# Adding raw x to ten blocks of the state at fold time, and storing those blocks straight from the state

## The chip, the cores and the metric

The kernel runs on one core of a Trainium2 chip. The metric is the time of one execution on the device in microseconds (us), the median of three runs. Engines are named as the profile names them: PE is the matrix engine and PEld its weight loads, DVE the vector engine, ACT the scalar engine, POOL the GpSimd engine, and SP the engine that issues all of this kernel's DMAs. Each engine works through its own queue of instructions in order.

## What is computed

Two branches read the same 2048 x 448 input, and their sum is added to it:

```python
def reference(A_x, A_w_r, A_w_i, B_x, B_w1, B_w2, B_w3, B_w4):
    def _A_ref(x, w_r, w_i):
        X = rfft2(x) * (w_r + 1j * w_i)
        return irfft2(X, s=(S, D))
    def _B_ref(x, w1, w2, w3, w4):
        h = _gelu(_layernorm(x, axis=-1) @ w1)
        hs = concatenate([four shifts of quarters of h], axis=-1) @ w2
        x1 = x + hs
        h2 = _gelu(_layernorm(x1, axis=-1) @ w3) @ w4
        return x1 + h2
    x = A_x
    xn = _layernorm(x, axis=-1)
    return x + _A_ref(xn, A_w_r, A_w_i) + _B_ref(xn, B_w1, B_w2, B_w3, B_w4)
```

Here S is 2048, D is 448 and the hidden width of the second MLP is 1792. B_x is not read. What matters for the change is the last line: raw x is one of three terms of the result, and terms may be added in any order as long as each is in the right scale.

## The kernel before

**Tiling.** The 2048 rows are cut into 16 blocks of 128 rows, row a*16+b being row a of block b. Each block has a slot of 128 x 448 floats in SBUF, `xb(b)`, which lives in the four tiles `xt`. It starts as x, is normalised in place, and from then on holds the running sum of the result: this is the state. To keep the half-precision matmuls in range, the state of blocks 0 to 11 is carried in a scaled form until the end; the factor `p12` (a column of the small tile `s12`) turns it back, and what is added to it on the way is multiplied to match: `p34[:,0:1]` is the scale for adding the MLP's result to a scaled state, `p34[:,1:2]` the one for adding it to an unscaled row, and `sc[:,1:2]` the one for adding the spectral result to a scaled state.

**Stages.** First the token mixing (w1, shifts, w2), to about 98 us. Then the channel MLP, in eight groups G of two blocks, each in seven steps fp. A step has a `front` (22 matmuls at L433 into a bank `pw`, the gelu at L763, the split of the result into two halves `hf` by ACT at L767 and DVE at L768) and a `back` (12 or more matmuls at L798 and L809 into the accumulators); fronts run up to two steps ahead of backs. After the last step DVE adds the accumulator to the state (L818). The MLP is the filler of the whole second part of the kernel: the spectral branch is laid into it. That branch has a fold stage (`do_fold`, about 98 to 186 us), a stage of 16 spectral chunks (about 190 to 270 us) and an inverse stage (about 280 to 381 us).

**The fold stage** goes by pairs of blocks b0 = 0, 2, ..., 14. For each pair SP loads the raw x again into a buffer `xf` of which there are three (L571), ACT normalises it in place (L575, L576), POOL folds it with four additions through `xr` (L580 to L583), ACT and DVE split it into halves `xh` (L591, L592), PE transforms it (`step1`, L601), and ACT and DVE copy the result out of its bank (L605, L606). On POOL the fold shares the queue with `w4_forms` (L897 to L901), which prepares weights.

**The inverse stage** goes over the blocks in the order 12 to 15, 8 to 11, 0 to 7. `gather_u` and `inv_a` (L716 to L739) prepare a block, and `inv_b` multiplies it (L746) and adds it to the state on DVE (L747). For blocks below 12, `finish` follows: raw x is loaded a third time into one of two rows of `xr` (L556), DVE forms state * p12 + x there (L557), and SP stores the row (L561). Because there are two rows, a load waits until the store two blocks earlier is done. Blocks 12 to 15 get their raw x in a separate place ahead of the last two MLP groups, also by L556 and L557, and are stored at the very end.

**Order.** Nobody writes the order of the queues out by hand. A planner simulates the engines and puts ready instructions into the queues by priority: the MLP's matmuls have the lowest (`FILL`), its evacuations the highest (`EVAC`), the rest lies between in the order of the program. `with behind(key)` holds an instruction back, in the plan, until the instructions that were recorded under that key have been issued. `("f", G, fp)` is the split of `front(G, fp)` on ACT and DVE, `("m", G, fp)` the last matmul of `back(G, fp)`. `FOLD[b0 // 2]` is such a key for each pair: (0,5), (1,0), (1,1), (1,3), (1,4), (1,6), (2,0), (2,2).

Of the kernel before, what the change touches and what calls it, by code (L numbers as in the profile page):

```python
# [16 lines left out]
ALU = mybir.AluOpType  # L17
AX = mybir.AxisListType

S, D, DF, F = 2048, 448, 225, 1792  # L20
# [15 lines left out]
WMAX = [(1, 4), (1, 5), (2, 0), (2, 0), (2, 1), (2, 2), (2, 3), (2, 4)]  # L36
LATE = [(2, 2), (2, 3), (2, 4), (2, 5)]
HS = 3
STR = (5, 6, 7)
INV, LAG = 4, 2  # L40
EVAC, FILL = 0, 100000
# [81 lines left out]
def body(tc, nc, x, wf, w1, w2, w3, w4, c_g, c_n, c_small, out):  # L123
# [41 lines left out]
    def xb(b):  # L165
        g, i = WHERE[b]
        return xt[g][:, i]
# [385 lines left out]
    def unscaled(b, t=None):  # L553
        if t is None:
            t = row()[:, :D]
        SY.dma_start(t, xv[:, b])  # L556
        V.scalar_tensor_tensor(out=t, in0=xb(b), scalar=p12, in1=t, op0=ALU.mult, op1=ALU.add)  # L557
        return t

    def finish(b):  # L560
        SY.dma_start(ov[:, b], unscaled(b))  # L561


    OFF = [0, 113, 225, 338, 450]
    FAM = [0, 2, 1, 3]
    folds = {}

    def do_fold(b0):
        f = pfd.tile([128, 2, 4, 113], F32, tag="xf", bufs=3, name=f"xf{b0}")
        X = f.rearrange("p b s d -> p (b s d)")[:, 0:2 * D + 2].rearrange("p (b d) -> p b d", b=2)  # L570
        after["X", b0] = (SY.dma_start(X[:, :, 0:D], xv[:, b0:b0 + 2]).ins,)  # L571
        with behind("f", *FOLD[b0 // 2]):
            for i in range(2):
                x_ = X[:, i, 0:D]
                A.activation(out=x_, in_=x_, func=AF.Identity, scale=xn_scale[b0 + i], bias=xn_bias[b0 + i])  # L575
            A.activation(out=X[:, :, D:D + 1], in_=X[:, :, 0:1], func=AF.Copy)  # L576
        ad = X[:, :, 0:D].rearrange("p b (h d) -> p h b d", h=2)[:, :, :, 0:113]
        bc = X[:, :, 1:D + 1].rearrange("p b (h d) -> p h b d", h=2)[:, ::-1, :, 223:110:-1]
        u = xr.rearrange("p (a b s d) -> p a b s d", a=2, b=2, s=2)
        P.tensor_tensor(out=u[:, 0], in0=ad, in1=bc, op=ALU.add)  # L580
        P.tensor_tensor(out=u[:, 1], in0=ad, in1=bc, op=ALU.subtract)
        for k, op in ((0, ALU.add), (2, ALU.subtract)):
            i = P.tensor_tensor(out=f[:, :, k:k + 2].rearrange("p b s d -> p s b d"), in0=u[:, :, 0], in1=u[:, :, 1], op=op)  # L583
        after["fold", b0] = (i.ins,)
        for i in range(2):
            folds[b0 + i] = f[:, i].rearrange("p s d -> p (s d)")
# [33 lines left out]
    def w_scale_end(wm):  # L620
        t = pc.tile([128, 4], F32, name="wt")
        V.tensor_reduce(out=t[:, 0:1], in_=wm, axis=AX.X, op=ALU.max)
        pt = bank("sp", "wpt")
        T.transpose(pt[0:1, 0:128], t[:, 0:1], ident)
        V.tensor_reduce(out=t[0:1, 1:2], in_=pt[0:1, 0:128], axis=AX.X, op=ALU.max)
        V.tensor_scalar(out=t[0:1, 1:2], in0=t[0:1, 1:2], scalar1=2.0 ** -20, scalar2=None, op0=ALU.max)
        pb = bank("sp", "wpb")
        T.matmul(pb[:, 0:1], ones[0:1], t[0:1, 1:2], start=True, stop=True)
        e = pc.tile([128, 3], I32, name="we")
        V.tensor_copy(out=t[:, 2:3], in_=pb[:, 0:1])  # L630
        V.tensor_single_scalar(e[:, 0:1], t.bitcast(I32)[:, 2:3], 0x7F800000, op=ALU.bitwise_and)
        V.tensor_single_scalar(e[:, 1:2], e[:, 0:1], 0x7F800000, op=ALU.bitwise_xor)
        V.tensor_scalar(out=sc[:, 0:1], in0=e.bitcast(F32)[:, 1:2], scalar1=ZPRE, scalar2=None, op0=ALU.mult)
        for h in range(2):
            V.tensor_scalar(out=sc[64 * h:64 * h + 64, 2:3], in0=sc[64 * h:64 * h + 64, 0:1], scalar1=2.0 * h - 1.0,
                            scalar2=None, op0=ALU.mult)
        V.tensor_scalar(out=sc[:, 1:2], in0=e.bitcast(F32)[:, 0:1], scalar1=2.0 ** -21 / (ZPRE * UPRE * VPRE),
                        scalar2=s12[:, 0:1], op0=ALU.mult, op1=ALU.mult)


    stream, pfs, zs = {}, {}, {}
# [100 lines left out]
    def inv_b(b):  # L742
        vh = vhs.pop(b)
        py = bank("sp", f"py{b}")
        for n, (vi, ri) in enumerate(PASS):
            T.matmul(py[:, :D], cV[ri], vh[:, vi], start=n == 0, stop=n == 2)  # L746
        V.scalar_tensor_tensor(out=xb(b), in0=py[:, :D], scalar=sc[:, 1:2], in1=xb(b), op0=ALU.mult, op1=ALU.add)  # L747


    acc, xs, hs, hg, rest = {}, {}, {}, {}, {}  # L750
# [27 lines left out]
    def back(G, fp):  # L778
        h = hs.pop((G, fp))
        n = D // 2  # L780
        end = 4 if G == 7 else 6
        if fp == 0:
            acc[G] = [bank("acc", f"acc{G}{i}") for i in range(2)]
            if G in STR:
                xs[G] = [bank("tr", f"cr{G}{i}") for i in range(2)]
        if (G, fp) == (7, 5):
            xs[G] = [bank("tr", f"end{i}") for i in range(2)]
        C = [[(slice(0, D), acc[G][i][:, 0:D], 0, 6)] for i in range(2)]
        if G == 7:
            C[1] = [(slice(0, D), acc[G][1][:, 0:D], 0, 4)]  # L790
            if fp > 4:
                C[1] = [(slice(n * k, n * k + n), xs[G][k][:, 0:n], 5, 6) for k in range(2)]
        for i in range(2):
            for r, to, s, e in C[i]:
                with behind("m", G, fp) if (G, fp) == (7, 6) and ("m", G, fp) in after else contextlib.nullcontext():
                    for f in range(2):
                        for hi, wi in ((0, 0),) if crossed(G, fp) else ((0, 0), (0, 1), (1, 0)):
                            m = T.matmul(to, h[:, hi, 2 * f + i], w4p[0][:, wi, 2 * fp + f, r],  # L798
                                         start=fp == s and f == 0 and hi + wi == 0, stop=fp == e and f == 1 and hi == 1)
                after["m", G, fp] = (m.ins,)  # L800
        if crossed(G, fp):
            g = hg.pop((G, fp))
            X = [xs[G][k // 2][:, n * (k % 2):n * (k % 2) + n] for k in range(4)]
            H = [[acc[G][i][:, n * k:n * k + n] for k in range(2)] for i in range(2)]
            forms = [(0, 1, X[0], 9), (1, 3, H[1][0], 9), (3, 2, H[0][0], C[0][0][3]), (6, 4, X[2], 9),
                     (4, 5, X[3], end), (5, 6, X[1], end), (2, 7, H[1][1], C[1][0][3])]
            for hi, wi in ((0, 1), (1, 0)):
                for k, slot, to, e in forms:
                    m = T.matmul(to, h[:, hi, slot] if slot < 4 else g[:, hi, slot - 4], w4f[fp][k][wi], start=k in (0, 6) and fp == 0 and hi == 0,  # L809
                                 stop=hi == 1 and fp == e)  # L810
            after["m", G, fp] = (m.ins,)
        k34 = p34[:, 1:2] if G >= 6 else p34[:, 0:1]
        to = {i: rest[2 * G + i] if G >= 6 else xb(2 * G + i) for i in range(2)} if fp >= 4 else {}

        def evacuate(i):
            for r, src, _, e in C[i]:
                if fp == e:
                    V.scalar_tensor_tensor(out=to[i][:, r], in0=src, scalar=k34, in1=to[i][:, r], op0=ALU.mult, op1=ALU.add)  # L818
                    if G == 7 and fp == 6:
                        SY.dma_start(ov[:, 2 * G + i, r], to[i][:, r])  # L820

        with prio(EVAC):
            if G in STR and fp == end:
                e0, e1 = cross[:, 0], cross[:, 1]
                for i in range(2):
                    A.activation(out=cross[:, i], in_=xs[G][i][:, 0:D], func=AF.Copy, scale=k34)
                for o, x, y in ((e0[:, n:], e0[:, 0:n], e0[:, n:]), (e1[:, 0:n], e1[:, 0:n], e0[:, n:]),
                                (e0[:, n:], e0[:, n:], e1[:, n:]), (e1[:, n:], e1[:, 0:n], e1[:, n:])):
                    (V if G == 7 else P).tensor_tensor(out=o, in0=x, in1=y, op=ALU.add)
            for i in range(2):  # L830
                evacuate(i)
                if G in STR and fp == end:
                    (V if G == 7 else P).tensor_tensor(out=to[i], in0=to[i], in1=cross[:, 1 - i], op=ALU.add)
                if G == 6 and fp == 6:
                    SY.dma_start(ov[:, 2 * G + i], to[i])
# [235 lines left out]
    xh_buf = [pfd.tile([128, 2 * 452 + 16], F16, name=f"xh{i}") for i in range(4)]  # L1071
    for i in range(4):
        P.memset(xh_buf[i][:, 904:], 0.0)
    mlp([1, 2], ahead=AH, tags=("mm", "tr"))
    for b in range(0, NB, 2):
        do_fold(b)
        step1_in(b)
        step1_in(b + 1)
        with behind("m", *PACE[b // 2]):
            step1(b)  # L1080
            step1(b + 1)
# [74 lines left out]
```

## Time and profile before

| what | value |
|---|---|
| median of three runs | 410.98 us (409.61, 410.98, 411.87) |
| the profiled execution | 411.11 us, of which the profile's span is 409.2 us |
| granted clock of the matrix engine | 1.0 throughout |
| busy share of the span: PE, DVE, ACT, POOL | 98%, 77%, 66%, 40% |
| share of the chain that ended last: PE, DVE, ACT, DMA | 68%, 12%, 7%, 6% |

The chain is followed backwards from the last instruction, at each step to what released it. Busy shares are means over stages with different limits, so the views that follow are read stage by stage. A row of the timeline has the start in us, the duration in us, the engine, the line of the kernel, the operation, the tiles written and read, shapes, and a count; a bracket at its end gives the engine's idle time before the row and what ended it. A row with a count above one is a run of instructions whose duration reaches from the first start to the last end.

### The profile page before, as it was taken

The numbers are of one execution on the slowest core, as the hardware profiler recorded it, in microseconds if no ns is written. First come the engines' busy times: TensorE is split into PE (matmuls) and PEld (weight loads), VectorE is DVE, ScalarE is ACT, GpSimd is POOL, SyncE is SP. The second block draws the span as 40 slices with busy tenths as digits, with TensorE's granted clock in tenths as the row PEclk, the third lists the DMA queues.
The fourth block names the chain that finished last, engine by engine and source line by source line (L and its number), as shares of the span: only waits on it lengthen the run. The fifth ranks groups of instructions, "written<-read, shape, count | busy, mean of one in ns | idle before, by whom it ended". The sixth has DMA issues, their size and how long they took to land.

```text
span 409.2 us, 8827 instructions
## 1 busy us (share of the span) xinstructions
PE 402.4 (98%) x3379; PEld 295.4 (72%) x3379; DVE 313.3 (77%) x674; ACT 268.2 (66%) x465; POOL 164.1 (40%) x260
## 2 busy tenths in 40 slices
PE   8999999999999999999999999999999999999996
PEld 3554555666677877677878887877788888878885
DVE  5989998898654737975899988841698969898645
ACT  4699993984838766754788888757566555644332
POOL 3889820002297745599321212100133234434300
PEclk9999999999999999999999999999999999999999
DMA  8999999907710356527367567320000202332201
GB/s 280 352 264 181 170 178 259 270 2 156 159 48 0 94 207 198 158 24 179 94 173 157 144 149 181 98 60 2 1 2 2 69 22 77 107 108 76 88 2 45
DMA packets 57209, 49.46 MB, mean 121 GB/s; under 512 B 41312, under 2 KB 52192, under 8 KB 57168
## 3 DMA queue, kind: packets, MB, share of 16 engines
q1 hardware_dynamic: 57168, 48.91, 46.3%
q8 instruction: 26, 0.43, 0.4%
q14 instruction: 15, 0.12, 0.1%
HBM read 35.06 MB, written 3.67 MB: 95 GB/s over the span
## 4 chain that ended last, share of the span: by engine, by line
PE 68%; DVE 12%; ACT 7%; DMA 6%; issue 3%; POOL 1%; SPq 0%; ACTq 0%; DVEq 0%; POOLq 0%
PE pw L433 23%; PE acc L798 18%; PE pw L462 6%; PE pw L507 6%; PE cr L809 3%; DMA wl<-wf 2%; PE acc L809 2%; ACT te L680 2%; PE ps L601 2%; PE py L746 2%; PE pe L724 2%; DVE te L683 1%; DVE te L681 1%; PE pu L704 1%; DMA h<-hs 1%
## 5 line engine op out<-in xcount | busy, mean ns | idle before, releaser
L433 PE MATMUL pw<-x2mem,w3p 128*128 128x256 f16 x1232 | 151.4, 272 | 0.0
L433 PEld LDWEIGHTS <-w3p 128*128 128x128 f16 x1232 | 118.8, 98 | 18.4
L798 PE MATMUL acc<-w4p,hf 128*128 128x448 f16 x508 | 106.7, 352 | 0.2 <-DVE xt L818 0.2
L798 PEld LDWEIGHTS <-hf 128*128 128x128 f16 x532 | 51.6, 98 | 37.1 <-issue 0.4
L768 DVE SCALAR_TENSOR_TENSOR hf<-pw,h,hf 128x512 f16<-128x512 f32 x56 | 41.8, 747 | 35.3 <-ACT hf L767 35.0
L763 ACT ACTIVATE pw<-pw,pe 128x512 f32<-128x512 f32 x56 | 36.7, 655 | 42.5 <-PE pw L433 42.4
L731 POOL TENSOR_TENSOR e<-e 128x226 f32<-128x226 f32 x16 | 12.8, 801 | 72.0 <-ACT e L728 67.9
L767 ACT ACTIVATE hf<-pw,h 128x512 f16<-128x512 f32 x56 | 38.3, 685 | 1.3
L507 PE MATMUL pw<-w2p,h 112*128 112x448 f16 x192 | 38.9, 352 | 0.1
L685 POOL TENSOR_TENSOR xr<-te 128x450 f32<-128x450 f32 x16 | 16.2, 1012 | 56.5 <-DVE te L683 50.6
L462 PE MATMUL pw<-w1p,w4x 128*128 128x448 f16 x176 | 34.9, 352 | 0.5 <-DVE h L936 0.5
L507 PEld LDWEIGHTS <-h 112*128 112x128 f16 x192 | 18.5, 98 | 16.8 <-DMA h<-x2mem 0.8
L462 PEld LDWEIGHTS <-w4x 128*128 128x128 f16 x176 | 17.0, 98 | 16.5 <-ACT w4x L422 0.7
L728 ACT ACTIVATE e<-pe 128x452 f32<-128x452 f32 x16 | 8.7, 544 | 20.7 <-PE pe L724 20.7
L580 POOL TENSOR_TENSOR xr<-xf 128x452 f32<-128x452 f32 x8 | 8.9, 1109 | 27.0 <-issue 16.0
L716 ACT ACTIVATE U<-y 113x512 f16<-113x512 f16 x32 | 18.0, 619 | 0.0
L592 DVE TENSOR_TENSOR xh<-xf,xh 128x452 f16<-128x452 f32 x16 | 14.0, 907 | 5.0 <-ACT xh L591 5.0
L680 ACT ACTIVATE te<-px 64x450 f32<-64x450 f32 x32 | 17.3, 539 | 0.6
L583 POOL TENSOR_TENSOR xf<-xr 128x452 f32<-128x452 f32 x16 | 16.7, 1066 | 0.6
L809 PE MATMUL cr<-w4x,hg 128*128 128x224 f16 x102 | 15.8, 259 | 0.1
L809 PEld LDWEIGHTS <-hg 128*128 128x128 f16 x152 | 14.7, 98 | 1.2 <-DVE hg L772 0.5
L738 ACT ACTIVATE vh<-e 128x448 f16<-128x448 f32 x16 | 9.2, 573 | 8.8 <-DVE e L736 8.8
(201 smaller groups left out, 773.1 us busy)
## 6 DMA issues: line engine op xcount, KB each, us to landing
wc<-wf SPq DMA_DIRECT2D x32, 225.0 KB, 3.7
wl<-wf SPq DMA_DIRECT2D x8, 450.0 KB, 3.7
xf<-x SPq DMA_DIRECT2D x8, 448.0 KB, 3.6
xt<-x SPq DMA_DIRECT2D x3, 896.0 KB, 11.0
w3raw<-w SPq DMA_DIRECT2D x3, 896.0 KB, 14.4
xr<-x SPq DMA_DIRECT2D x12, 224.0 KB, 2.6
out<-xr SPq DMA_DIRECT2D x12, 224.0 KB, 2.0
gn<-c_g SPq DMA_DIRECT2D x16, 128.0 KB, 3.3
```

The costliest lines, as they stand in the source:

```text
L433: T.matmul(ps_out, wp[:, wi + t, cols], xT[:, xi + t, tok], start=t == 0 and wi + xi == 0, stop=t == 3 and wi == 4)
L462: m = T.matmul(pm[:, :D], xTs[g][:, xi + t, 128 * i:128 * i + 128], w1p[:, wi + t], start=t == 0 and p == 0, stop=t == 3 and p == 2)
L507: m = T.matmul(w2b[b][:, :D], hT[g][:112, 4 * hi + k, o:o + 128], w2p[:, wi, k], start=k == 2 and hi + wi == 0, stop=k == 3 and hi == 1)
L583: i = P.tensor_tensor(out=f[:, :, k:k + 2].rearrange("p b s d -> p s b d"), in0=u[:, :, 0], in1=u[:, :, 1], op=op)
L680: i = A.activation(out=e[64 * h:64 * h + 64], in_=px_[64 - 64 * h:128 - 64 * h, :2 * DF], func=AF.Copy)
L685: P.tensor_tensor(out=z, in0=t[:, 0], in1=t[:, 1], op=ALU.add)
L716: A.activation(out=U[b][:113, p].rearrange("p q (c k) -> p q c k", c=NC), in_=Y1[:113, p, :, :, b], func=AF.Copy)
L763: A.activation(out=pm, in_=pm, func=AF.Gelu_apprx_tanh, scale=r3)
L767: i = A.activation(out=h[:, 0], in_=pv_, func=AF.Copy, scale=h3)
L768: j = V.scalar_tensor_tensor(out=h[:, 1], in0=pv_, scalar=h3, in1=h[:, 0], op0=ALU.mult, op1=ALU.subtract)
L798: m = T.matmul(to, h[:, hi, 2 * f + i], w4p[0][:, wi, 2 * fp + f, r], start=fp == s and f == 0 and hi + wi == 0, stop=fp == e and f == 1 a ...
L809: m = T.matmul(to, h[:, hi, slot] if slot < 4 else g[:, hi, slot - 4], w4f[fp][k][wi], start=k in (0, 6) and fp == 0 and hi == 0, stop=hi ...
```

## The change

For the pairs 2, 4, 6, 8 and 10, that is blocks 2 to 11, raw x is added to the state when it has been loaded for the fold, and before ACT overwrites it in place. The state of these ten blocks is from then on unscaled, and what is added later takes other scales: `p34[:,1:2]` in place of `p34[:,0:1]`, and a new column `sc[:,3:4]` in place of `sc[:,1:2]`. At the end they are stored from `xb(b)`. Blocks 0 and 1 keep the old way, since their MLP group is done before, and so do blocks 12 to 15. The load of a pair is taken out of `do_fold` into `load_fold`; for the first three pairs it stands in the program ahead of the MLP's groups 1 and 2, with its additions held behind `("f", 0, 6)`; for the others it stands where it stood, and the additions take the pair's own key in `FOLD`.

```diff
+EARLY = (2, 4, 6, 8, 10)
...
     def finish(b):
-        SY.dma_start(ov[:, b], unscaled(b))
+        SY.dma_start(ov[:, b], xb(b) if b // 2 * 2 in EARLY else unscaled(b))
...
-    def do_fold(b0):
+    Xs = {}
+
+    def load_fold(b0, pin):
         f = pfd.tile([128, 2, 4, 113], F32, tag="xf", bufs=3, name=f"xf{b0}")
         X = f.rearrange("p b s d -> p (b s d)")[:, 0:2 * D + 2].rearrange("p (b d) -> p b d", b=2)
         after["X", b0] = (SY.dma_start(X[:, :, 0:D], xv[:, b0:b0 + 2]).ins,)
+        Xs[b0] = f, X
+        if b0 in EARLY:
+            with behind("f", *pin):
+                for i in range(2):
+                    V.scalar_tensor_tensor(out=xb(b0 + i), in0=xb(b0 + i), scalar=p12, in1=X[:, i, 0:D], op0=ALU.mult, op1=ALU.add)
+
+    def do_fold(b0):
+        f, X = Xs.pop(b0)
         with behind("f", *FOLD[b0 // 2]):
...
+        V.tensor_tensor(out=sc[:, 3:4], in0=sc[:, 1:2], in1=p12, op=ALU.mult)
...
-        V.scalar_tensor_tensor(out=xb(b), in0=py[:, :D], scalar=sc[:, 1:2], in1=xb(b), op0=ALU.mult, op1=ALU.add)
+        V.scalar_tensor_tensor(out=xb(b), in0=py[:, :D], scalar=sc[:, 3:4] if b // 2 * 2 in EARLY else sc[:, 1:2], in1=xb(b),
+                               op0=ALU.mult, op1=ALU.add)
...
-        k34 = p34[:, 1:2] if G >= 6 else p34[:, 0:1]
+        k34 = p34[:, 1:2] if G else p34[:, 0:1]
...
+    for b in (0, 2, 4):
+        load_fold(b, (0, 6))
     mlp([1, 2], ahead=AH, tags=("mm", "tr"))
     for b in range(0, NB, 2):
+        if b > 4:
+            load_fold(b, FOLD[b // 2])
         do_fold(b)
```

## The prediction

> **What bounds the kernel now.** I read the page's busy times first, then the busy times of stretches of 10 us, then single stretches of the timeline, engine by engine.
>
> ```profile
> PE 402.4 (98%) x3379; PEld 295.4 (72%) x3379; DVE 313.3 (77%) x674; ACT 268.2 (66%) x465; POOL 164.1 (40%) x260
> ```
>
> PE is busy for all but 6.8 us of the 409.2 us span. A busy PE may still be waiting inside, so its pace has to be looked at. Here is a piece of the timeline of PE in the fold stage:
>
> ```profile
> 145.37 2.56 PE L433 MATMUL pw<-x2mem,w3p 128*128 128x256 f16 x22
> 147.77 2.43 PE L798 MATMUL acc<-w4p,hf 128*128 128x448 f16 x12
> 150.04 1.50 PE L601 MATMUL ps<-csm,xh 128*128 128x128 f16 x24
> ```
>
> From start to start, 22 matmuls of 256 columns take 2.40 us, 109 ns each, and 12 of 448 columns take 2.27 us, 189 ns each: 0.42 ns a column in both. The groups follow each other without a hole. Where the rows look like this, nothing that another engine does faster can shorten the run; only holes can be won. The stretches show where holes are (PE, PEld, DVE, ACT, POOL, then clock and DMA):
>
> ```profile
> 160.00:170.00 10.00, 9.78 (x83) 6.99 (x82) 10.00 (x15) 7.13 (x13) 4.17 (x4) 1.00 0.52 153
> 210.00:220.00 10.00, 9.82 (x116) 8.13 (x114) 9.36 (x16) 8.51 (x17) 1.96 (x2) 1.00 0.61 141
> 240.00:250.00 10.00, 9.72 (x103) 7.75 (x102) 9.15 (x16) 9.38 (x17) 2.21 (x2) 1.00 0.71 180
> 340.00:350.00 10.00, 9.80 (x105) 8.26 (x104) 8.55 (x18) 4.87 (x9) 3.20 (x5) 1.00 0.30 93
> 350.00:360.00 10.00, 9.93 (x90) 7.70 (x89) 10.00 (x27) 6.14 (x11) 3.95 (x4) 1.00 0.36 117
> ```
>
> Visible holes from 160 us on: 0.22 + 0.18 + 0.28 = 0.68 us up to 250 us, and 0.20 + 0.07 = 0.27 us in the inverse stage, where DVE is full. A hole shorter than about 0.16 us doesn't show, since a matmul of 256 columns is drawn with 0.27 us (two of them in 0.38 us) though its place is 0.109 us. The end is this:
>
> ```profile
> 405.44 1.00 DVE L818 SCALAR_TENSOR_TENSOR x2mem<-end,p,x2mem 128x224 f32<-128x224 f32 x2
> 405.54 1.31 SPq L820 DMA_DIRECT2D out<-x2mem  x3
> ```
>
> The last evacuation and the last stores belong to block 15, which the change doesn't touch. So the tail behind the last matmul stays as it is, and in the part that the change touches, from about 113 us on, the kernel is bound by PE's own work.
>
> **What is removed.** Ten of the twelve additions of L557 and ten of the twelve loads of L556 in the inverse stage, and with them the waits on SP for a free row.
>
> ```profile
> L557 DVE SCALAR_TENSOR_TENSOR xr<-xt,s,xr x12: 670/686/1557, 319.2 to 379.1; 128x448 f32<-128x448 f32 x12
> L556 SPq DMA_DIRECT2D xr<-x x12: 327/328/340, 265.1 to 374.1; - x12
> ```
>
> At the median of 0.686 us ten additions are 6.9 us of DVE, at the shortest 6.7 and at the longest 15.6. The loads are ten times 0.33 us of SP, and nothing but L557 waits for them. This is engine time, not run time. What it is worth is read from the holes of PE in the inverse stage; these rows give the three large ones, with the DVE rows around them:
>
> ```profile
> 341.61 0.67 DVE L557 SCALAR_TENSOR_TENSOR xr<-xt,s,xr 128x448 f32<-128x448 f32 x1
> 342.20 0.67 DVE L747 SCALAR_TENSOR_TENSOR xt<-py,sc,xt 128x448 f32<-128x448 f32 x1
> ...
> 341.91 0.82 PE L433 MATMUL pw<-x2mem,w3p 128*128 128x256 f16 x6
> 342.93 0.73 PE L746 MATMUL py<-vh,csm 128*128 128x448 f16 x3 [0.20 <-DVE xt L747]
> ...
> 349.07 0.69 DVE L557 SCALAR_TENSOR_TENSOR xr<-xt,s,xr 128x448 f32<-128x448 f32 x1 [1.41 <-DMA xr<-x]
> ...
> 350.83 0.45 PE L809 MATMUL cr<-w4x,hg 128*128 128x224 f16 x3
> 351.29 0.27 PE L809 MATMUL acc<-w4p,hg 128*128 128x224 f16 x1
> ...
> 356.46 1.00 DVE L557 SCALAR_TENSOR_TENSOR xr<-xt,s,xr 128x448 f32<-128x448 f32 x1
> ...
> 357.83 0.60 PE L433 MATMUL pw<-x2mem,w3p 128*128 128x256 f16 x4
> 358.49 0.27 PE L809 MATMUL cr<-w4x,hg 128*128 128x224 f16 x1
> ```
>
> Six matmuls from 341.91 should end their places at 342.56 (6 x 0.109); the next starts at 342.93, so 0.37 us are lost. Three of 224 columns from 350.83 need 0.28 us; 351.29 is 0.18 us late. Four from 357.83 need 0.44 us; 358.49 is 0.22 us late. Together 0.77 us, and each time a DVE queue that had an L557 in it up to two microseconds before (once with 1.41 us of waiting for a reload) delivered late. The row at 349.07 belongs to block 0, which keeps its addition; but with only two rows ever asked for, both loads go out before the inverse stage (the first row of L556 is at 265.1), so that wait goes too. What is late next: DVE still has the four e additions, hf, hg and L747 of every block, so I don't take the whole 0.77. Bounds: 0 and 0.77; I take 0.6, nearer the upper one, as all three holes have an L557 just ahead.
>
> **What is added.** Ten additions of two SBUF operands in the fold stage, of the same shape as L557, and one operation on a single column. The column's nearest row is this:
>
> ```profile
> 195.86 0.20 DVE L637 TENSOR_SCALAR sc<-we,s 128x1 f32<-128x1 f32 x1
> ```
>
> It comes after the column that the chunks need, and nobody waits for it before 280 us; at worst 0.2 us. The first four additions (blocks 2 to 5) stand in DVE's queue behind the split of step (0,6). The stretch, by engine:
>
> ```profile
> 112.66 0.75 DVE L768 SCALAR_TENSOR_TENSOR hf<-pw,h,hf 128x512 f16<-128x512 f32 x1 [3.79 <-ACT hf L767]
> 114.44 1.79 DVE L592 TENSOR_TENSOR xh<-xf,xh 128x452 f16<-128x452 f32 x2 [1.02 <-ACT xh L591]
> 117.74 1.44 DVE L818 SCALAR_TENSOR_TENSOR xt<-acc,p,xt 128x448 f32<-128x448 f32 x2 [1.51 <-PE acc L798]
> ...
> 113.75 1.03 POOL L897 TENSOR_TENSOR w4x<-w4p 128x448 f16<-128x448 f16 x1
> ...
> 118.29 1.50 PE L601 MATMUL ps<-csm,xh 128*128 128x128 f16 x24
> ...
> 126.40 2.43 PE L798 MATMUL acc<-w4p,hf 128*128 128x448 f16 x12
> ```
>
> The split ends at 113.41. The four additions then hold DVE, at s us each, until 113.41 + 4s, and behind them stand L592 for the first fold pair (1.79 us for two, 0.90 each), then L818 (its accumulators are written again at 126.40, over 6 us later). PE's L601 at 118.29 needs block 0's half, and block 1's from its twelfth matmul on, at 118.96. So the first is in time as long as 113.41 + 4s + 0.90 is below 118.29, s below 0.995; the second as long as 113.41 + 4s + 1.79 is below 118.96, s below 0.94. The size of s is the term in dispute. POOL reads SBUF all through this stretch. The same two L592 are the nearest row, with POOL beside them:
>
> ```profile
> L592 DVE TENSOR_TENSOR xh<-xf,xh x16: 611/834/1487, 114.4 to 175.1; 128x452 f16<-128x452 f32 x16
> ```
>
> Alone an L592 takes 0.611 us, here 0.90: 0.29 us for POOL beside it. For an addition that is 0.670 + 0.29 = 0.96 us, a cost of 4 x (0.96 - 0.94) = 0.08 us. Bounds: none at 0.670, and 4 x (1.557 - 0.94) = 2.5 us at the longest L557. I take 0.1.
>
> The Trainium skill (page "SBUF — State Buffer", section "Who interferes with whom") says that a DVE instruction with two SBUF inputs and a GpSimd instruction that reads SBUF exclude each other for a whole instruction, the later one blocked until the earlier ends. It speaks against putting these additions beside POOL's work; the trace has the effect, but at 0.29 us on the mean of two, not at a whole POOL operation each.
>
> The other six stand behind the splits of (1,3), (1,4) and (1,6), and ACT's normalising of the pair, which overwrites x in place, now waits for them:
>
> ```profile
> 132.69 0.75 DVE L768 SCALAR_TENSOR_TENSOR hf<-pw,h,hf 128x512 f16<-128x512 f32 x1 [0.34 <-ACT hf L767]
> 134.78 2.51 DVE L592 TENSOR_TENSOR xh<-xf,xh 128x452 f16<-128x452 f32 x2 [1.34 <-ACT xh L591]
> 138.70 0.75 DVE L768 SCALAR_TENSOR_TENSOR hf<-pw,h,hf 128x512 f16<-128x512 f32 x1 [0.21 <-ACT hf L767]
> ...
> 132.55 1.41 ACT L575 ACTIVATE xf<-xf,nm,vw 128x448 f32<-128x448 f32 x2
> 138.56 1.40 ACT L575 ACTIVATE xf<-xf,nm,vw 128x448 f32<-128x448 f32 x2
> ...
> 139.90 1.50 PE L601 MATMUL ps<-csm,xh 128*128 128x128 f16 x24
> 156.05 1.50 PE L601 MATMUL ps<-csm,xh 128*128 128x128 f16 x24
> ...
> 132.41 0.37 SPq L571 DMA_DIRECT2D xf<-x  x1
> ```
>
> For pair 6 two additions run from 133.44 to 134.8 or 135.4, and ACT's L575 slips from 132.55 to at most 134.4, where the second waits for the second addition; behind it on ACT stand L591 of pair 4 and the next gelu, 2 us late at most. L592 of pair 4 then ends at about 139.3 instead of 137.29, and PE asks for it at 139.90: covered, with 0.6 us to spare. If that cover were gone, the price would be what L592 is late, up to 2 us. For pair 8 the split ends at 139.45, and one addition later, at 140.1 to 140.4, ACT can start the L575 that stands at 138.56 now, up to 1.9 us late; the pair's transform is the one at 156.05, so there is room for much more than that. The split hf that is made at 138.70 is used by the back that starts at 147.77, so ACT and DVE may be 8 us late there. The pair's load is issued at 132.41, and loads of this kind take 3.6 us:
>
> ```profile
> xf<-x SPq DMA_DIRECT2D x8, 448.0 KB, 3.6
> ```
>
> so x is there at 136.0, before the split. Pair 10 stands behind (1,6), where DVE is half idle. I cost these six at nothing. POOL, slowed beside them, has only the folds, whose cover is the same, and weight forms that are first used in group 5.
>
> SP's part: the first three loads go out at the same point of its queue as now, right when the memory is free; no DMA is moved past another. Ten stores that waited for L557 now wait for L747.
>
> **The sum.** -0.6 + 0.1 = -0.5 us. The profiled execution took 411.11 us (span 409.2, so 1.9 around it), 0.13 above the median of 410.98. Forecast: 410.98 - 0.5, rounded, 410.5 us.
>
> **The rivals.**
>
> *DVE's queue at 113 us decides (slower).* The four additions collide with POOL so that each sits out a POOL operation (1.03 us in the row at 113.75) and then works for 0.67: s = 1.70. PE then waits 4 x (1.70 - 0.94) = 3.0 us before L601, from s = 0.94 on. That gives 410.98 + 3.0 - 0.6 = 413.4 us. For it: POOL is full there, and the longest L557 took 1.557 us. Against: it is one of twelve, and the planner can put other matmuls ahead of L601. It would slow the run by over 2 us from s = 1.6 on. This is also what the Trainium skill's rule gives, taken word for word.
>
> *It was hidden anyway.* The holes at 342, 351 and 358 us come from the length of the chain POOL, DVE, ACT, DVE of each inverse block, and without L557 the next block's work takes its place. For it: L747 is only one of the releases named. Against: DVE is the only full engine there. 411.0 us.
>
> *The plan comes out otherwise (faster).* All queues behind 113 us are planned anew. If the new order also closes the holes at 160, 210 and 240 us, each with the 0.16 us that it can hide, 0.68 + 3 x 0.16 + 0.77 = 1.93 us go: 409.1 us, and every hole too short to be seen would add to that. Nothing in the profile says that it will; a reshuffle can open such holes as well, which I count to the first rival's side.
>
> **How the numbers follow.** Forecast 0.40; hidden anyway 0.21; the slower side 0.23; the better plan 0.16. That last case ends just short of the bound by the holes that can be seen, and those that can't lie beyond it, so I count 0.12 of it as past the bound. A difference under 0.5%, 2.05 us, can't be told from none here: the three runs lie 2.26 us apart. Slower by more: 0.23, the slower rival. Faster by more: 0.12 out of the better plan. Within: 0.65. The range goes from 408.5 (the better plan and half a microsecond of unseen holes) to 413.4 (the slower rival).
>
> **What would show it.** Right: ten L557 rows gone, ten new rows on DVE between 113 and 153 us of 0.67 to 1.0 us each, L601's first start not later than 118.3, DVE under 9 of 10 us at 350 to 360, and the three holes closed. Wrong: new rows of 1.5 us, a PE wait ahead of L601 or on hf in 113 to 160 us, or PE holes past 160 us that sum to more than 2 us; a gain over 1.5 us would mean that PE's pace has holes which I didn't see.

## The result and the profile after

The changed kernel takes 414.21 us, the median of eight runs (412.46 to 417.08), against 410.89 us for the kernel before, the median of eight runs beside them. The ratio is 1.0081, with a 95% interval of 1.0063 to 1.0099: slower by 3.3 us, and outside the range that was given, 408.5 to 413.4. The profiled execution is the slowest of the eight, 417.08 us with a span of 415.1, so holes in it are at the upper end of what the runs have.

The busy line of the changed kernel's page, and then the first line of its list of PE's waits (who waited for what; us in total, times, the longest):

```profile
PE 404.3 (97%) x3379; PEld 296.6 (71%) x3379; DVE 316.9 (76%) x675; ACT 267.6 (64%) x465; POOL 162.0 (39%) x260
```

```profile
PE acc L811 <- DVE xt L831: 3.0, 1, 3.0
```

PE ran the same 3379 matmuls. One wait stands out, 3.0 us long: the first back of group 2 (L811, which was L798) waits for L831 (which was L818), the addition of group 1's accumulator to the state. (Line numbers of the changed kernel are 1 to 13 higher.) Around that place the stretches of 5 us look like this:

```profile
160.00:165.00 5.00, 5.00 (x39) 3.62 (x38) 3.60 (x5) 2.91 (x6) 4.29 (x5) 1.00 0.55 163
165.00:170.00 5.00, 2.00 (x15) 1.29 (x14) 5.00 (x8) 4.43 (x9) 0.52 (x1) 1.00 0.65 207
170.00:175.00 5.00, 5.00 (x34) 3.27 (x33) 5.00 (x7) 0.00 (x0) 4.92 (x5) 0.66 0.33 95
```

PE works 2.00 of 5 us while DVE is full, and in the next 5 us it is busy but at a granted clock of 0.66. The queue of DVE, and then PE, in the timeline:

```profile
159.66 1.09 DVE L269 TENSOR_REDUCE wm<-wl 128x1 f32<-128x900 f32 x1 [3.77 <-DMA wl<-wf]
161.43 1.09 DVE L269 TENSOR_REDUCE wm<-wl 128x1 f32<-128x900 f32 x1 [0.68 <-DMA wl<-wf]
162.44 0.74 DVE L781 SCALAR_TENSOR_TENSOR hf<-pw,h,hf 128x512 f16<-128x512 f32 x1
163.89 1.09 DVE L269 TENSOR_REDUCE wm<-wl 128x1 f32<-128x900 f32 x1 [0.72 <-DMA wl<-wf]
164.90 1.28 DVE L617 TENSOR_TENSOR y<-ps,y 128x512 f16<-128x512 f32 x2
166.16 1.09 DVE L269 TENSOR_REDUCE wm<-wl 128x1 f32<-128x900 f32 x1
167.16 1.16 DVE L603 TENSOR_TENSOR xh<-xf,xh 128x452 f16<-128x452 f32 x2
168.24 0.68 DVE L831 SCALAR_TENSOR_TENSOR xt<-acc,p,xt 128x448 f32<-128x448 f32 x1
...
161.14 2.43 PE L811 MATMUL acc<-w4p,hf 128*128 128x448 f16 x12
163.41 2.57 PE L434 MATMUL pw<-x2mem,w3p 128*128 128x256 f16 x22
168.97 1.29 PE L811 MATMUL acc<-w4p,hf 128*128 128x448 f16 x6 [3.00 <-DVE xt L831]
```

The accumulators are complete at about 163.4. L831 could run then, but four absmax instructions (L269, the largest values of the spectral weights), two copies (L617) and the split L603 of fold pair 10 stand ahead of it in DVE's queue. Three of the four absmaxes wait for their loads. The tile wl has two halves, so the third load goes out only when the first absmax is done. PE needs the accumulators at 165.8 and gets them at 168.97.

In the kernel before, the same four absmaxes, copies and split stand ahead of L818, but the first load is there earlier, and PE loses 0.38 us at this place:

```profile
154.47 1.09 DVE L268 TENSOR_REDUCE wm<-wl 128x1 f32<-128x900 f32 x1 [2.24 <-DMA wl<-wf]
...
164.12 0.67 DVE L818 SCALAR_TENSOR_TENSOR xt<-acc,p,xt 128x448 f32<-128x448 f32 x1
...
164.84 1.29 PE L798 MATMUL acc<-w4p,hf 128*128 128x448 f16 x6 [0.22 <-DVE xt L818]
```

To see all that PE lost, also what the modelled ends hide, I took for each matmul the distance to the start of the next and subtracted its place, 0.417 ns a column of the moving operand plus 2 ns (that makes 109 ns for 256 columns, as the prediction read off). The sum of the rest is PE's holes. It accounts for everything: span less holes is 396.8 to 397.1 us in all fourteen profiled executions of this study. The table gives the holes in us, by stretch of the span, for the kernels before and after and for the runs that follow:

```
                        0-100  112-125  155-190  190-275  275-292  338-365    all   span
before                   7.38     0.06     0.70     2.12     0.11     1.10  12.28  409.2
after                    8.36     0.44     4.98     2.09     0.78     0.65  18.19  415.1
remove_only              6.62     0.06     0.69     2.07     0.79     0.68  11.64  408.7
add_only                 6.53     0.52     2.52     2.08     0.79     0.69  13.99  410.9
first_four               8.16     0.52     0.34     2.07     0.79     0.84  13.51  410.5
last_six                 6.93     0.06     5.31     2.62     0.77     0.64  17.15  413.9
pin_x12                  7.83     0.50     1.44     3.02     0.78     0.65  15.02  412.1
absmax_later             7.40     0.43     1.48     2.08     0.79     0.65  13.62  410.7
adds_earlier             7.30     0.47     1.34     2.07     0.80     0.66  13.42  410.5
both edits               7.33     0.57     0.84     2.09     0.80     0.65  13.06  410.1
remove_gathers_later     7.48     0.06     1.61     2.05     0.12     0.66  12.73  409.8
all_pins_a               7.44     0.06     1.45     2.03     0.12     0.67  12.53  409.6
all_pins_b               6.34     0.06     0.19     3.87     0.13     0.69  12.00  409.0
all_pins_c               8.17     0.05     0.84     2.05     0.12     0.67  12.66  409.7
```

The first column is the part ahead of the change; it differs by up to 2 us between single executions, so spans are not compared without it. The rest of the row for after says where the two executions differ: 0.38 us more at the first fold pair, 4.28 us more at group 1's evacuation and behind it (1.6 of it in matmuls that ran at the lower clock), 0.67 us more at 287 us, and 0.45 us less in the inverse stage. What makes the last two is a question for the experiments.

How did the loads come late? The path is in these rows of the changed kernel, on DVE, ACT and POOL first for pair 6 and then for pair 8, and behind them on DVE and SP (SPq is SP issuing a DMA):

```profile
134.70 1.86 DVE L579 SCALAR_TENSOR_TENSOR xt<-xt,s,xf 128x448 f32<-128x448 f32 x2
...
136.00 0.76 ACT L586 ACTIVATE xf<-xf,nm,vw 128x448 f32<-128x448 f32 x1 [2.00 <-DVE xt L579]
138.09 0.75 ACT L586 ACTIVATE xf<-xf,nm,vw 128x448 f32<-128x448 f32 x1
...
139.54 1.06 POOL L591 TENSOR_TENSOR xr<-xf 128x452 f32<-128x452 f32 x1 [4.06 <-issue]
...
141.38 2.05 DVE L579 SCALAR_TENSOR_TENSOR xt<-xt,s,xf 128x448 f32<-128x448 f32 x2
142.14 0.76 ACT L586 ACTIVATE xf<-xf,nm,vw 128x448 f32<-128x448 f32 x1 [1.46 <-DVE xt L579]
143.46 0.76 ACT L586 ACTIVATE xf<-xf,nm,vw 128x448 f32<-128x448 f32 x1 [0.56 <-DVE xt L579]
145.42 1.07 POOL L591 TENSOR_TENSOR xr<-xf 128x452 f32<-128x452 f32 x1 [1.14 <-issue]
...
150.81 1.17 DVE L603 TENSOR_TENSOR xh<-xf,xh 128x452 f16<-128x452 f32 x2 [1.77 <-ACT xh L602]
...
152.04 0.38 SPq L574 DMA_DIRECT2D xf<-x  x1
152.47 0.94 SPq L626 DMA_DIRECT2D wl<-wf  x2
```

ACT idles 2.00 us until the first addition of pair 6 is done, and the normalising of its second block comes only at 138.09, behind other work that was planned between the two. POOL starts folding pair 6 at 139.54. By then this execution is 1.34 us behind the one before (the split of step (1,3) starts at 134.03 instead of 132.69; 0.38 us of it lost at the first fold pair and the rest ahead of the change), so of the 5.2 us against 134.33 before, 3.9 arise behind that point. Pair 8 is held back by additions of its own as well: ACT waits 1.46 us for the first and 0.56 us for the second, and POOL starts that fold at 145.42 instead of 141.13. The last use of pair 8's buffer (L603) then starts at 150.81 instead of 146.22. That buffer is the one that the x load of pair 14 waits for. SP issues it at 152.04 instead of 147.92, and the loads wl stand behind it: 152.47 instead of 148.38. The absmaxes, L831 and PE follow.

### The profile page after: what moved, and what is told of

It reads as the page before. It is cut to its first block, busy times and chain, and to the rows that moved or that the text cites. A ratio compares the mean times of both kernels' runs of the same rounds, so it can differ in the third digit from the quotient of the medians.

```text
span 415.1 us, 8810 instructions
## 1 busy us (share of the span) xinstructions
PE 404.3 (97%) x3379; PEld 296.6 (71%) x3379; DVE 316.9 (76%) x675; ACT 267.6 (64%) x465; POOL 162.0 (39%) x260
## 4 chain that ended last, share of the span: by engine, by line
PE 48%; ACT 6%; DVE 5%; DMA 2%; issue 2%; POOL 0%; SPq 0%; DVEq 0%; ACTq 0%; POOLq 0%
PE pw L434 19%; PE acc L811 13%; PE cr L822 3%; PE acc L822 2%; DMA wl<-wf 2%; PE py L758 2%; PE pe L736 2%; PE pu L716 2%; PE pp L670 1%; PE px L687 1%; ACT te L692 1%; PE ps L612 1%; ACT U L728 1%; ACT zb L704 1%; ACT y L719 1%
## 5 line engine op out<-in xcount | busy, mean ns | idle before, releaser
L811 PE MATMUL acc<-w4p,hf 128*128 128x448 f16 x508 | 107.6, 353 | 3.5 <-DVE xt L831 3.0
L811 PEld LDWEIGHTS <-hf 128*128 128x128 f16 x532 | 51.6, 98 | 40.4 <-issue 3.6
L743 POOL TENSOR_TENSOR e<-e 128x226 f32<-128x226 f32 x16 | 11.0, 688 | 70.5 <-ACT e L740 66.3
L603 DVE TENSOR_TENSOR xh<-xf,xh 128x452 f16<-128x452 f32 x16 | 14.9, 970 | 3.3 <-ACT xh L602 3.3
L616 ACT ACTIVATE y<-ps 128x512 f16<-128x512 f32 x16 | 9.1, 587 | 10.8 <-PE ps L612 10.6
L745 DVE TENSOR_TENSOR e<-e 128x113 f32<-128x113 f32 x16 | 9.6, 599 | 8.2 <-POOL e L743 8.2
L751 DVE TENSOR_TENSOR vh<-e,vh 128x448 f16<-128x448 f32 x16 | 9.9, 622 | 7.4 <-ACT vh L750 7.4
```

## The experiments

Each was run in rounds beside the kernel before, and the medians of before are those of its own call: 410.81 us for the first four runs, 410.41 for the next four, 410.28 for the three after them and 410.38 for the last.

**Where the wl loads stand in the plan.** In the kernel the loads are held behind the x load of pair 14.

```diff
-    with behind("X", 14):
+    with behind("X", 12):
         wm = w_scale()
```

> The changed kernel, but the loads of the spectral weights' largest values (wl) are held in the plan behind the x load of pair 12 instead of pair 14. Theory A: the additions hold back the folds of pairs 6 and 8, so the buffer for pair 14 comes free late, its load blocks SP's queue with the eight wl loads behind it, the absmax instructions that wait for them block DVE's queue, and group 1's evacuation behind them keeps PE waiting (3.0 us at 165.8). Then this kernel has its first wl load before 149 us, a hole under 0.6 us ahead of group 2's first back, granted clock 1.0 in the stretch 170 to 175, and 410.4 to 411.5 us. Theory B: the DVE time of the additions itself (9.35 us over the ten rows) makes the loss; then the hole stays over 2 us and the time is 413.5 to 414.5.

Measured: 413.42 us, ratio 1.0072 (1.0055 to 1.0088). The first wl load goes out at 148.49, the hole falls to 1.13 us, and no drop of the clock follows. But the hole is not under the 0.6 us that theory A gave, and the time is 1.9 us above theory A's range and 0.08 us under theory B's; 0.93 us of it the new plan lost among the chunks (3.02 against 2.09). From this kernel's rows of SP and DVE:

```profile
148.49 0.88 SPq L626 DMA_DIRECT2D wl<-wf  x2
...
163.60 2.38 DVE L603 TENSOR_TENSOR xh<-xf,xh 128x452 f16<-128x452 f32 x2 [0.31 <-ACT xh L602]
165.91 0.67 DVE L831 SCALAR_TENSOR_TENSOR xt<-acc,p,xt 128x448 f32<-128x448 f32 x1
```

What now stands ahead of L831 is the split of pair 10. It is late because ACT waits 3.56 us for that pair's additions, which in this plan start at 155.92, behind an absmax that itself waits 1.71 us for its load. Theory A lacked that second part; with it I call it A2. As it stood, theory A failed in the time and in the hole; theory B failed in the hole (over 2 us) and came near in the time.

**The removal alone.** The additions are taken out of `load_fold`.

> The changed kernel with the ten additions left out, so that raw x is missing from ten blocks and their state stays scaled; the reloads and additions at the end are gone all the same. Theory A and B: no hole over 0.6 us at group 1's evacuation, 410.0 to 410.9 us, which is the worth of the removal alone (prediction: 0.6 us, bounds 0 and 0.77). Theory C: the loss comes from the new plan at the end (0.64 us at 287, 0.43 at 348) and not from the additions; then over 412.5.

Measured: 411.17 us, ratio 1.0005 (0.9986 to 1.0023). The hole at group 1's evacuation is 0.38 us as before. The inverse stage has 0.42 us less of holes, but one of 0.64 us appears at 281 us; this kernel has no additions, so they aren't needed for it. The expected gain did not come. Up to 196 us all queues are in the order of the kernel before; the first entry that differs is the new column's operation on DVE, 0.16 us long.

**The additions alone.** `finish` loads and adds for all twelve blocks again.

> The changed kernel with the additions in the fold stage, and with the reload and addition at the end for all twelve blocks as before, so that raw x comes into ten blocks twice. Theory A and B: the hole of about 3 us ahead of group 2's first back stays, and 414.0 to 415.2 us. Theory C: 410.5 to 411.5.

Measured: 413.00 us, ratio 1.0069 (1.0051 to 1.0087), a hole of 2.36 us ahead of group 2's first back. The place is as theory A and B had it, the time 1.0 us under the expected range. So the additions carry the loss.

The run answers a second question too. It removes nothing: all twelve reloads and their additions are there (L558 here, L557 before), and from the split at 281 us on, every queue holds the same entries in the same order as in the kernel before. Still its inverse stage has only 0.69 us of holes, as little as with the removal (0.65 to 0.68), and the hole at 283 us is there as well (0.64). So the removal is needed for neither. The first two rows are from add_only, the third is from the changed kernel:

```profile
L558 DVE SCALAR_TENSOR_TENSOR xr<-xt,s,xr x12: 669/685/1554, 321.3 to 380.8; 128x448 f32<-128x448 f32 x12
345.02 0.73 PE L758 MATMUL py<-vh,csm 128*128 128x448 f16 x3 [0.20 <-DVE xt L759]
...
348.58 0.73 PE L758 MATMUL py<-vh,csm 128*128 128x448 f16 x3 [0.26 <-DVE xt L759]
```

The largest of the three holes that the prediction read (0.37 us) is 0.36 us with twelve additions and 0.43 us with two. The other two, 0.18 and 0.22 us, are absent in add_only, with the same additions in the same places of the queues.

**Four or six of the ten.** `EARLY = (2, 4)`, and then `EARLY = (6, 8, 10)`, with `k34` to match.

> The changed kernel with the early addition for pairs 2 and 4 alone. Theory A: pairs 6 and 8 are not held back, the x load of pair 14 is issued before 149.5 us, the hole ahead of group 2's first back is under 0.8 us, and the time is 410.6 to 411.6. Theory B: 4.2 of 9.35 us of additions remain, so about 0.45 of the loss, 412.0 to 412.8.

> The changed kernel with the early addition for pairs 6, 8 and 10 alone. Theory A2: no hole at the first pair's transform (0.06 us in 112 to 125 us as before), the hole ahead of group 2's first back stays at 2 to 3.2 us, and 412.2 to 414.0. Theory B: 5.2 of 9.35 us of additions remain, 412.2 to 412.9, with the holes spread.

Measured: first_four 411.82 us, 1.0033 (1.0019 to 1.0046), last_six 412.94 us, 1.0055 (1.0034 to 1.0075). With the first four alone the hole at group 1's evacuation is gone altogether (0.34 in the column 155-190, under the 0.70 before), and 0.46 us are lost at the first pair. The load of pair 14 went out at 149.18. With the last six alone it is the other way round: nothing at the first pair, and 3.50 us at the evacuation. The loss sits in one place in each and isn't spread with the amount of additions. The time of first_four is 0.2 us over what theory A gave and 0.2 us under what theory B gave; the new hole at 281 to 287 us is in it too. The time of last_six lies in theory A2's range and 0.04 us over theory B's, and its hole is 0.3 us over. So it is the places that part the theories here, not the times.

**What stands in DVE's queue.** Only the keys of two absmaxes are moved.

```diff
-WMAX = [(1, 4), (1, 5), (2, 0), (2, 0), (2, 1), (2, 2), (2, 3), (2, 4)]
+WMAX = [(1, 4), (1, 5), (2, 1), (2, 1), (2, 1), (2, 2), (2, 3), (2, 4)]
```

> The changed kernel with the second, third and fourth... more exactly: the keys of the third and fourth absmax moved from (2,0) to (2,1), so that in DVE's queue one absmax stands between the last addition and group 1's evacuation instead of four. Loads and additions as in the changed kernel. Theory A2 (the hole ahead of group 2's first back is made in DVE's queue, by absmaxes that wait for late loads and by pair 10's late split xh, both ahead of the evacuation): the hole falls from 2.4 to 3.2 us to 0.5 to 1.5 us, what pair 10's split still holds, and the time is 412.0 to 413.2. Theory B (the DVE time of the additions as such): hole and time as in the changed kernel, 412.5 to 414.5, the hole over 2 us.

Measured: 411.94 us, ratio 1.0032 (1.0018 to 1.0047). Ten additions, the same loads, the first wl still at 151.54, and the evacuation comes in time:

```profile
161.75 2.66 DVE L603 TENSOR_TENSOR xh<-xf,xh 128x452 f16<-128x452 f32 x2
164.34 0.67 DVE L831 SCALAR_TENSOR_TENSOR xt<-acc,p,xt 128x448 f32<-128x448 f32 x1
165.59 2.07 DVE L269 TENSOR_REDUCE wm<-wl 128x1 f32<-128x900 f32 x2
```

Of the hole 0.20 us are left at the first and 0.37 at the second half of the back, less than expected. A new one of 0.76 us stands at 174 us: the loads of the fifth and sixth absmax can go out only when the moved third and fourth are done, so the fifth and sixth now stand late, at 170.01 and 171.95, ahead of a copy L617 that a transform waits for. The time is 0.06 us under the range expected.

**When the additions run.** Pair 6's go behind (1,1), pair 10's behind (1,5).

```diff
-            load_fold(b, FOLD[b // 2])
+            load_fold(b, {6: (1, 1), 8: (1, 4), 10: (1, 5)}.get(b, FOLD[b // 2]))
```

> The changed kernel with the additions of pair 6 behind (1,1) instead of (1,3), and those of pair 10 behind (1,5) instead of (1,6), that is one or two steps ahead of the pair's normalising, which then has not to wait for them. The same ten additions run. Theory A2: pairs 6 and 10 are not held back, the x load of pair 14 goes out at least 1.5 us earlier than in the changed kernel, the hole ahead of group 2's first back is under 1.2 us, and the time 411.3 to 412.5. Theory B: same DVE time, so no change, 412.5 to 414.5.

> Both edits together. Theory A2: nothing late stands ahead of group 1's evacuation, the hole ahead of group 2's first back is under 0.4 us, and what is left over the kernel before is 0.4 at the first four additions and 0.7 at 282 to 288 us less 0.45 in the inverse stage: 411.0 to 411.9. Theory B: 412.5 to 414.5.

Measured: adds_earlier 411.97 us, 1.0036 (1.0023 to 1.0050), with a hole of 1.18 us; both edits 411.65 us, 1.0026 (1.0014 to 1.0039), with no hole over 0.1 us at the evacuation. In adds_earlier the x load of pair 14 goes out at 149.88, 2.2 us earlier, of which 1.0 is the earlier start of the whole stretch (its first addition is at 113.26 instead of 114.29); so 1.1, less than the 1.5 expected. What still stands ahead of L831 is two late absmaxes:

```profile
161.52 1.09 DVE L269 TENSOR_REDUCE wm<-wl 128x1 f32<-128x900 f32 x1 [0.77 <-DMA wl<-wf]
163.66 1.08 DVE L269 TENSOR_REDUCE wm<-wl 128x1 f32<-128x900 f32 x1
165.26 0.68 DVE L831 SCALAR_TENSOR_TENSOR xt<-acc,p,xt 128x448 f32<-128x448 f32 x1
```

With both edits what remains is 0.5 us at the first pair, 0.7 at 282, 0.7 at 174, less 0.45 in the inverse stage. Theory B falls with these three runs: the ten additions are all there, and the times lie under its 412.5 us.

**The hole at 281 us.** In remove_only ACT does four gathers between a gelu and the split that PE waits for. Two blocks' gathers are held back:

```diff
-                gather_u(bs[n])
+                with behind("f", 4, 4) if n in (2, 3) else contextlib.nullcontext():
+                    gather_u(bs[n])
```

> The kernel remove_only (additions left out, raw x missing from ten blocks), with the gathers of the third and fourth block of the inverse stage (L724 there) held behind the split of step (4,4), so that ACT does not do them ahead of that split. Theory D: the removal closes 0.45 us of holes in the inverse stage and the new plan opens 0.68 us at 281 us, by those gathers; with them later the 0.64 us hole is gone and the time is 0.3 to 0.7 us under the kernel before. Rival: the removal is worth nothing in any plan; then the time is that of the kernel before, within 0.2 us, and another hole opens.

Measured: 409.91 us, ratio 0.9997 (0.9985 to 1.0009). The hole at 281 us is gone (0.12 in its column), so the order of the gathers makes it; a gain of 0.3 to 0.7 us is not shown, as the interval includes none. In the profiled execution a hole of 1.14 us stands at 164.6, where remove_only has 0.38. Up to 277 us all five queues hold the same instructions in the same order in both kernels, so the hole at group 1's evacuation differs between executions of one order, here by 0.76 us, and a difference of that size between two profiles shows nothing by itself. A worth of the removal is not shown: its own stage has 0.65 to 0.68 us of holes with two of the twelve reloads left, 0.84 with eight (first_four) and 0.69 with all of them (add_only), and the times show no gain.

**All of it.** The first four additions go behind (0,5), where DVE idles 3.8 us, together with the keys above. The diff is to the changed kernel; its three lines WMAX belong to all_pins_a, all_pins_b and all_pins_c in this order, and in all_pins_b the gathers go behind (4, 5).

```diff
     for b in (0, 2, 4):
-        load_fold(b, (0, 6))
+        load_fold(b, (0, 5))
...
+            load_fold(b, {6: (1, 1), 8: (1, 4), 10: (1, 5)}.get(b, FOLD[b // 2]))
...
+WMAX = [(1, 4), (1, 5), (2, 1), (2, 1), (2, 1), (2, 2), (2, 3), (2, 4)]
+WMAX = [(1, 4), (1, 5), (2, 1), (2, 1), (2, 2), (2, 3), (2, 4), (2, 5)]
+WMAX = [(1, 4), (1, 5), (2, 1), (2, 1), (2, 2), (2, 2), (2, 3), (2, 4)]
...
+                with behind("f", 4, 4) if n in (2, 3) else contextlib.nullcontext():
+                    gather_u(bs[n])
```

> The changed kernel with four edits of its keys: the first four additions behind (0,5) instead of (0,6), pairs 6 and 10 behind (1,1) and (1,5), the third and fourth absmax behind (2,1), and the gathers of the third and fourth block behind (4,4). All ten additions run and nothing is left out. Theory A2 with D: no hole at the first pair's transform (0.06 us in 112 to 125), none ahead of group 2's first back, none at 282; a hole of about 0.6 stays at 174. Time 0 to 0.6 us under the kernel before. Theory B: the additions' DVE time costs wherever it lies, so 1 to 3 us over.

> As all_pins_a, with the fifth to eighth absmax one step later as well, so that one absmax instead of two stands ahead of the copy that the transform at 174 us waits for, and the gathers behind (4,5), where the new plan has them. Theory A2 with D: no hole of over 0.3 us from 112 to 180 us; 0.4 to 1.2 us under the kernel before. Theory B: 1 to 3 us over.

> As all_pins_a, with only the fifth absmax one step later, behind (2,2), so that one absmax instead of two stands ahead of the copy that the transform at 174 us waits for. PE's order is that of all_pins_a. Theory A2 with D: the 0.77 us hole at 174 goes, no other opens, and the time is 0.4 to 1.0 us under the kernel before. Rival (the hole at 174 is made by POOL's or ACT's lateness): hole and time as in all_pins_a.

Measured: all_pins_a 410.12 us, 0.9993 (0.9981 to 1.0005); all_pins_b 411.57 us, 1.0029 (1.0018 to 1.0040); all_pins_c 410.50 us, 0.9999 (0.9985 to 1.0013). From all_pins_a, the summary of the ten additions, and DVE where the first four now run:

```profile
L579 DVE SCALAR_TENSOR_TENSOR xt<-xt,s,xf x10: 670/1372/1484, 108.9 to 146.8; 128x448 f32<-128x448 f32 x10
```

```profile
108.95 4.08 DVE L579 SCALAR_TENSOR_TENSOR xt<-xt,s,xf 128x448 f32<-128x448 f32 x4
112.95 0.74 DVE L781 SCALAR_TENSOR_TENSOR hf<-pw,h,hf 128x512 f16<-128x512 f32 x1
115.45 1.79 DVE L603 TENSOR_TENSOR xh<-xf,xh 128x452 f16<-128x452 f32 x2 [1.77 <-ACT xh L602]
```

All ten additions run, at a median of 1.37 us even longer than in the changed kernel, and the time is that of the kernel before. The loss of the change is undone by order alone, though holes of 0.16 and 0.37 us remain at group 2's first back, where none was expected. In all_pins_b moving four more absmaxes and the gathers closed the last holes up to 190 us and opened 1.8 us among the chunks (3.87 against 2.03). Its time, 1.3 us over the kernel before, lies in theory B's range, but its holes stand at 260 to 270 us, far from the additions. In all_pins_c the hole at 174 stayed at 0.67 us (0.77 in all_pins_a), the outcome that the rival there named. PE still waits there for the copy L617 on DVE (0.51 us), and the absmax that is left ahead of it waits 0.79 us for its load, so POOL or ACT isn't shown as the cause, and what makes the hole stays open. No version beat the kernel before beyond the noise.

## Why the prediction was wrong

- **What bounds the kernel: right.** PE's own work is 397 us in every execution, and time moves only with its holes. The tail kept its form.
- **The removal, -0.6 us (0 to 0.77): a term that no run shows.** Holes in the inverse stage went from 1.10 to 0.65 us, but in add_only, which removes nothing, they went to 0.69. I read the three holes off one execution and gave them to the L557 just ahead. The largest stayed without it (0.43 us), and the two small ones went also where all twelve stayed. DVE was not relieved as I said either: 9.25 of 10 us busy from 350 to 360, not under 9. The rival "hidden anyway" gave the right time for the removal alone; whether for its reason, that the next block's work takes the place, was not tested. The hole of 0.67 us at 281 to 287 us comes with the removal alone, with the additions alone and with both, as long as the gathers aren't held back. It belongs to the new plan, and which part of the edit makes that plan is open.
- **The first four additions, +0.1 us: mis-sized.** It is 0.38 us. Each took 1.04 us instead of 0.96 (4.17 us for four), and the two L603 behind them took 2.41 us instead of the 1.79 that I carried over from their row. They now run beside L910 and L912 on POOL; in last_six, without the first four additions, they take 1.78. That POOL's work is what slowed them was not tested. The place and the wait were right:

```profile
114.29 4.17 DVE L579 SCALAR_TENSOR_TENSOR xt<-xt,s,xf 128x448 f32<-128x448 f32 x4
118.38 2.41 DVE L603 TENSOR_TENSOR xh<-xf,xh 128x452 f16<-128x452 f32 x2
...
119.92 0.72 PE L612 MATMUL ps<-csm,xh 128*128 128x128 f16 x10
120.85 0.73 PE L612 MATMUL ps<-csm,xh 128*128 128x128 f16 x10 [0.21 <-DVE xh L603]
```

- **"I cost these six at nothing": the step that failed.** With the six alone the changed kernel is 2.3 us slower than the one before (last_six, ratio 1.0055), and in the profile of the changed kernel the place that they hold back lost 4.28 us. I asked only who waits for the split halves, and found PE's transforms with room to spare; they did have it. I did not follow the other thing that a late fold releases, its buffer. The x load of pair 14 waits for it, eight loads stand behind that load on SP, eight absmaxes on DVE wait for those, and group 1's evacuation stands behind four of them. "No DMA is moved past another" was the sentence that closed this off: none had to be moved, it was enough that one in front waited. My figure for ACT was also too small. I let it slip from 132.55 to 134.4; it came at 136.00 and 138.09 for the two blocks, 1.34 us of which this execution was behind anyway; the plan had put other work between them.
- **The slower rival** came nearest with its 413.4 us, but by luck, since it had the wrong place. Its loss at 113 us is 0.38 us, and additions that wait out a whole POOL operation were not seen: the rows between are 0.67 to 1.45 us.

```profile
L579 DVE SCALAR_TENSOR_TENSOR xt<-xt,s,xf x10: 671/961/1449, 114.3 to 153.8; 128x448 f32<-128x448 f32 x10
```

- **"A reshuffle can open such holes as well, which I count to the first rival's side":** it should have had its own price. Three plans of this study opened one without any work added in that place: 0.67 us at 281 to 287 (with the removal alone and with the additions alone), 0.93 us among the chunks (pin_x12), 1.8 us there (all_pins_b).

The kernel before already had this wait, 0.38 us at 164.4, and the row of its evacuation at the end of a full DVE stretch was in the views that I read (160 to 170 us, DVE 10.00 of 10). What remains open is how much each of the two late things, the absmaxes and pair 10's split, would cost alone in the changed kernel's plan, as each edit also made a new plan. The runs show no worth of the removal, but they don't exclude one of a few tenths of a microsecond.

## What to carry to other kernels

When work is put ahead of a buffer's last reader, follow the buffer, not only the result: ask which transfer waits for it, what stands behind that transfer in its queue, and who waits in order for those. Work for which its engine has room can still cost its whole lateness at the one place where an in-order queue already has no room, and a small wait that is there already (0.38 us here) marks that place. Where a planner makes the order, any edit is an edit of the whole plan, so a gain of a few tenths of a microsecond can't be counted on. And a hole of a few tenths that is read off one execution may belong to that execution: look for it in a second profile of the same order before counting on its removal.

## What the runs showed of the hardware

A long hole of PE was followed by a lower granted clock. In the changed kernel the hole of 3.16 us is followed by a clock of 0.66 over 5 us: twelve matmuls of 256 columns after 170 us are 0.10 us late each and two of 448 columns 0.18 us, 1.6 us together, and these are about twice their places. Past 100 us, the longest hole without a drop is the 2.36 us of add_only. These rows are from last_six (a hole of 3.50 us) and then from add_only:

```profile
165.00:170.00 5.00, 2.49 (x10) 1.28 (x10) 5.00 (x8) 3.16 (x6) 2.24 (x3) 0.80 0.50 170
170.00:175.00 5.00, 5.00 (x49) 3.90 (x48) 5.00 (x7) 1.18 (x2) 5.00 (x6) 0.86 0.45 121
```

```profile
165.00:170.00 5.00, 3.56 (x25) 2.40 (x25) 5.00 (x8) 3.22 (x6) 2.25 (x2) 1.00 0.51 144
```

The length of a single hole does not decide it, though. In all_pins_c the clock is 0.66 from 10 to 15 us, and 0.98 over the first 100 us, while the longest idle time that PE shows from 4 us to there is 1.07 us:

```profile
0.00:100.00 100.00, 97.08 (x546) 54.52 (x547) 88.06 (x255) 73.96 (x124) 44.50 (x123) 0.98 0.84 209
```

```profile
8.51 0.38 PE L926 MATMUL wps<-nma,ones 128*128 128x4 f32 x2 [1.07 <-DVE nma L346]
```

The Trainium skill (page "TensorE: Matmul & The Clock Gate", section "What's actually happening") has the clock go to half after an idle window of about 3.4 us that runs freely. The trace agrees with half, by the matmuls at twice their places; the hole of 3.16 us is a little shorter than the window named. Four of the changed kernel's eight runs have a mean clock of 0.995 or 0.996 over the span and took 414.22 to 417.08 us; the four at 1.000 took 412.46 to 414.20. That fits a hole that differs from run to run, and with it whether the clock drops, but only one of these runs has a trace, and in all_pins_c such a mean (0.996) comes from a drop at another place. So it isn't shown for the others.
